# One PSUM tile of eight banks for every piece, one normalization over two banks, and another written order

## The chip, the cores and the metric

The kernel runs on one core of a Trainium2 chip. The metric is the device time of one execution in microseconds. The engines are called PE (TensorE, matmuls and transposes), DVE (VectorE), ACT (ScalarE), POOL (GpSimd) and SP (SyncE, which only issues DMAs here). Each engine has its own instruction stream and works it off in order; between engines there are semaphores.

## The reference, cut to what matters

The inputs are q, k, v of shape (4, 8, 768, 64) and the weights of a mixture of attention experts: a gate (512, 4), and for each of 4 experts wq, wk, wv (512 x 64) and wo (64 x 512). All is float32, as is the output (4, 768, 512).

```python
# first attention: 8 heads; each row sees 8 global keys and the last 96
scores = (q @ k.T) / 8 + bias            # bias = -slope[h] * distance
scores = where(keep, scores, -1e9)
a = exp(scores - max(scores)); a = a / (sum(a) + 1e-9)
x = a @ v                                # heads side by side: (4, 768, 512)
# second: 4 experts, causal, the best 2 of 4 by the gate
logits = x @ w_gate                      # w: softmax over the best two
for e in range(4):
    s = (x @ wq[e]) @ (x @ wk[e]).T / 8  # causal
    a = softmax(s)
    out += w[e] * (a @ (x @ wv[e]) @ wo[e])   # where e is among the two
```

## The kernel before

The work is cut into 24 units: 4 batches of 6 blocks of 128 rows. A unit has some forty pieces, written `name-unit`, and each piece is one or a few instructions on one engine:

- `ldq`, `ldk` (for two units at a time), `ldv`: loads, issued by SP. `cq`, `ck`, `cv` cast them to float16 (POOL, but for the first q and k). `tq`, `tk` transpose on PE, `eq`, `ek` copy the result out of PSUM (DVE).
- First attention, in halves of four heads: `s0`, `s1` are the scores on PE (before, each in a tile of two PSUM banks), `x0`, `x1` the exponentials on ACT, `m0`, `m1` the multiplication by a table of decays and masks (`M`) on DVE. `z0`, `z1` multiply by v, which has a column of ones behind it, so that each head's row sum comes out as a 65th column. `r0`, `r1` take the reciprocals of the sums and `n0`, `n1` multiply by them, both on DVE, four heads at a time (lines 641 to 666).
- `kp`, `vp` put the eight global keys and values in the place of the first rows of a used buffer; `vp` is a small DMA.
- `tx`, `ex` transpose x. `pq`, `eqk` make and copy the second q and k, `pv`, `ev` the second v and the logits; `xr`, `mx`, `wr`, `zi` make the gate's weights.
- Second attention: `s20`, `s21`, `s22` scores, `x20` to `x22` exponentials, `af` the causal mask (POOL), `y2` the product, `rz`, `cw`, `n2` the normalization with the gate's weights, `tz`, `ez`, `po`, `eo` the output projection, `so` the store.

The order is written out; a search made it: the text `ORDER` lists all pieces, and `Stream.run` issues them in that order. A word such as `eqk-1*` takes the second engine in the piece's list, and the numbers behind a colon name PSUM slots. The dictionaries of engines and times in `add` were used by the search that made the order, and decide nothing when the kernel is built, apart from the engines' order in them.

PSUM is cut into two kinds of slots: two of two banks each for scores (`s`), and four of one bank (`w`) for everything else:

```python
    def wtile(shape, dt, name):
        return psum.tile(shape, dt, name=name, tag=f"w{st.slots[0]}")

    def stile(shape, name):
        return psum.tile(shape, F32, name=name, tag=f"s{st.slots[0]}")
...
    st = Stream({"s": 2, "w": 4})
```

Ahead of all work on data, PE runs 24 matmuls of 512 columns on a tile of zeros, `nil` (`warm`, line 489). At the end `good0` to `good2` test on DVE that all row sums lie in a range (`inside`, line 792), `total` adds the results up on PE, and `flag` hands the number to a branch: if a sum is out of range, a slow general path computes all again. It is not taken here.

Of the kernel before, what the change touches and what calls it, by code (L numbers as in the profile page):

```python
# [8 lines left out]
F32 = mybir.dt.float32  # L9
# [19 lines left out]
s1-4:1 rz-0 x0-4 ldk-6 pv-1:3 cw-0 kp-4 n2-0 ldq-8 n0-2 pq-1:2 x1-4 cq-6 n1-2 ldv-6 ones mx-1 ldk-8
m1-3 eqk-1* tq-6:1 tx-2:0 m1-4 w-o z0-3:2 ex-2 s20-1:1 r0-3 s0-5:0 m0-4 pq-2:0 xr-1 x0-5 wr-1 eq-6  # L30
ck-6 ev-1 n0-3 s1-5:0 eqk-2* z1-3:2 x20-1 vp-3 m0-5 tk-6:1 ldv-4 r1-3 tz-0:0 x1-5 pv-2:3 ldk-10 ek-6
af-1 n1-3 kg-6 s0-6:1 s1-6:0 ez-0 x0-6 m1-5 tx-3:2 po-0:0 x1-6 ldq-10 kp-6 m0-6 y2-1:1 ldq-12 xr-2
eo-0 cq-8 ex-3 s21-2:1 s0-7:0 rz-1 x21-2 mx-2 pq-3:2 zi-1 ldv-7 cw-1 x0-7 cv-6 ev-2* wr-2 tq-8:0
ck-8 n2-1 eqk-3* s1-7:1 eq-8 s20-2:0 x1-7 z0-6:1 tz-1:3 m1-6 tk-8:2 cv-4 r0-6 ez-1 x20-2 z1-6:0 n0-6
s20-3:1 vg-6 r1-6 z1-4:1 n1-6 po-1:3 ck-10 vp-6 ek-8 ldv-5 s21-3:0 eo-1 r1-4 tx-6:0 n1-4 pv-3:2
x20-3 kp-7 ex-6 z0-4:3 m0-7 tk-10:1 xr-3 ev-3 vp-4 cq-10 pq-6:0 r0-4 x21-3 n0-4 ek-10 tx-4:3 af-2
zi-2 ldk-12 mx-3 s0-8:1 ex-4 s1-8:0 cq-12 ldq-14 x0-8 eqk-6 pq-4:3 m1-7 so-1 tq-12:1 eqk-4* cv-7
wr-3 tq-10:0 eq-12 x1-8 s21-4:1 eq-10 cv-5 z0-7:1 z1-7:2 x21-4 r0-7 kp-8 s20-4:0 m1-8 vp-7 z0-5:0
ldv-8 z1-5:3 x20-4 r1-7 n0-7 s22-4:1 r0-5 n1-7 y2-2:1 ck-12 r1-5 x22-4 n0-5 tx-7:2 ldk-14 n1-5
s1-9:0 s20-6:1 rz-2 tx-5:3 x20-6 cw-2 ldv-9 ex-7 tk-12:0 ldq-16 x1-9 ex-5 cq-14 s0-9:1 ek-12 pq-5:2  # L40
x0-9 zi-3 n2-2 kp-9 af-4 pv-5:3 eqk-5* m0-8 s0-10:1 tq-14:1 xr-5 af-3 mx-5 x0-10 wr-5 pq-7:2 cv-8
eq-14 ev-5 m1-9 s21-5:0 eqk-7* s1-10:1 m0-10 z1-8:3 x21-5 z0-8:1 kp-10 r1-8 tz-2:2 kg-12 y2-3:0
ck-14 r0-8 vp-8 ez-2 x1-10 n1-8 ldv-10 pv-4:2 rz-3 n0-8 ldk-16 po-2:3 cw-3 ldv-12 cv-9 tx-8:1 n2-3
eo-2 s22-5:0 so-0 ex-8 s1-11:1 xr-4 ev-4 m0-9 tz-3:0 tk-14:3 x22-5 cq-16 mx-4 pq-8:1 ez-3 ek-14
x1-11 m1-10 s1-12:0 po-3:0 x1-12 af-6 eqk-8 z1-9:3 eo-3 s0-12:1 m1-12 s20-5:0 x0-12 wr-4 z0-9:1
pv-6:0 ck-16 zi-4 x20-5 r1-9 vp-9 r0-9 n1-9 y2-4:2 ldq-18 zi-5 n0-9 xr-6 so-2 ev-6 s21-8:1 rz-4
s0-11:0 af-5 mx-6 ldk-18 x21-8 wr-6 tx-9:3 tq-16:1 cw-4 ldv-11 x0-11 kp-12 ex-9 cv-10 tk-16:0 n2-4
eq-16 s20-8:1 ldv-13 s20-7:0 x20-8 m1-11 tz-4:2 pq-9:3 ez-4 ek-16 x20-7 af-8 z0-10:1 po-4:2 m0-11
eqk-9* y2-5:0 cq-18 r0-10 eo-4 n0-10 s1-13:1 rz-5 s21-9:0 cw-5 x1-13 cv-12 z1-10:1 n2-5 tq-18:2
vp-10 r1-10 m0-12 tz-5:3 x21-9 z1-12:0 ldq-20 n1-10 s0-13:1 ez-5 so-3 pv-7:1 kp-13 eq-18 ck-18 x0-13  # L50
ldk-20 po-5:3 r1-12 mx-7 ev-7* tx-10:2 xr-7 s1-14:0 zi-6 eo-5 wr-7 s0-14:1 vg-12 x1-14 zi-7 z0-12:1
ex-10 tk-18:3 af-7 vp-12 r0-12 n1-12 pq-10:2 so-5 cv-11 x0-14 ek-18 so-4 m1-13 s20-9:0 eqk-10*
z0-11:0 kg-18 n0-12 cv-13 pv-8:3 x20-9 r0-11 n0-11 tx-12:1 kp-14 z1-11:2 cq-20 mx-8 ex-12 y2-6:0
ldv-14 xr-8 s21-10:1 ev-8 rz-6 r1-11 s0-15:0 wr-8 x21-10 n1-11 y2-7:1 pq-12:3 rz-7 cw-6 cw-7 x0-15
n2-6 n2-7 tx-11:2 tq-20:0 m0-13 eqk-12* tz-7:1 s22-10:1 ex-11 s1-15:0 x22-10 ez-7 z1-13:3 kp-15
eq-20 z0-13:2 ck-20 x1-15 tz-6:1 vp-13 s1-16:1 r1-13 ez-6 n1-13 pq-11:0 ldv-15 x1-16 m0-14 ldq-22
ldv-16 po-7:1 cv-14 r0-13 eqk-11* n0-13 po-6:3 m1-14 eo-7 s21-11:0 s22-11:1 eo-6* x21-11 pv-9:1
m0-15 tx-13:2 so-6 z0-14:0 x22-11 mx-9 s0-16:0 r0-14 ex-13 pv-10:3 kp-16 n0-14 af-9 xr-9 x0-16
z1-14:2 wr-9 y2-8:0 ev-10* cv-15 vp-14 s20-10:1 r1-14 mx-10 ev-9 ldk-22 zi-8 n1-14 s1-17:0 xr-10
x20-10 ldv-19 zi-9 tk-20:1 rz-8 wr-10 so-7 cw-8 pq-13:2 m1-15 x1-17 af-10 n2-8 y2-9:3 ek-20 cq-22  # L60
eqk-13* tz-8:0 s20-11:0 ez-8 s1-18:1 rz-9 x20-11 tx-14:1 cw-9 cv-16 po-8:0 ex-14 z0-15:2 n2-9 x1-18
z1-15:1 r0-15 ck-22 tz-9:3 n0-15 eo-8 vp-15 s20-12:0 s0-17:1 r1-15 ez-9 pq-14:2 n1-15 so-8 x0-17
zi-10 m1-16 ldv-18 tq-22:3 x20-12 m0-16 po-9:0 eqk-14* m1-18 tk-22:1 eq-22 eo-9 s0-18:0 s20-13:1
m1-17 so-9 x0-18 z0-16:2 pv-11:3 ldv-17 x20-13 kp-18 ek-22 af-12 y2-10:0 mx-11 r0-16 xr-11 ev-11
cv-18 s21-14:0 wr-11 s20-14:1 x21-14 n0-16 tx-15:1 vg-18 ldv-22 z1-16:3 rz-10 x20-14 ex-15 s1-19:0
vp-16 r1-16 cw-10 pv-12:2 n1-16 x1-19 n2-10 s0-19:1 mx-12 m0-18 tx-16:3 tz-10:0 kp-19 pq-15:1 x0-19
m0-17 ez-10 ex-16 ev-12 s1-20:0 xr-12 eqk-15 s0-20:1 x1-20 po-10:0 kp-20 m1-19 z0-18:3 pq-16:1 cv-17
x0-20 wr-12 eo-10* af-14 z1-17:2 eqk-16* r0-18 so-10 s1-21:1 n0-18 af-11 s0-21:0 ldv-20 r1-17 x1-21
z0-17:3 n1-17 cv-19 z1-18:1 zi-11 y2-12:0 r0-17 y2-11:2 r1-18 vp-18 af-13 n0-17 x0-21 ldv-23 zi-12
rz-12 n1-18 kp-21 s21-15:1 rz-11 cw-12 pv-13:1 cw-11 x21-15 n2-12 tx-17:3 n2-11 tz-12:0 mx-13  # L70
s21-16:0 ev-13 ex-17 s20-15:1 xr-13 x21-16 ez-12 pq-17:3 wr-13 m0-19 x20-15 cv-20 tz-11:0 z1-19:2
ez-11 po-12:1 r1-19 m0-21 eqk-17* po-11:0 af-15 zi-13 eo-12 s22-16:0 n1-19 s20-16:1 eo-11* z0-19:3
x22-16 so-12 y2-13:1 cv-22 pv-14:2 r0-19 x20-16 so-11 rz-13 n0-19 tx-18:0 vp-19 cw-13 mx-14 s1-22:0
n2-13 xr-14 ldv-21 ev-14 s21-17:1 ex-18 x1-22 tz-13:3 tx-19:1 wr-14 pq-18:0 ez-13 m0-20 x21-17 m1-20
pv-15:3 y2-14:2 xr-15 ex-19 eqk-18* s22-17:1 zi-14 rz-14 s20-17:0 mx-15 cw-14 ev-15 wr-15 z0-20:1
x22-17 n2-14 z1-20:0 po-13:3 r0-20 r1-20 vp-20 n0-20 y2-15:2 zi-15 eo-13 n1-20 tz-14:1 rz-15 x20-17
# [785 lines left out]
```

## Time and profile before

| | |
|---|---|
| median of 3 runs | 146.87 us (146.66 to 147.22) |
| the profiled execution | 146.58 us, span 144.9 us |
| mean granted clock of PE | 0.964 |
| busy: PE, DVE, ACT, POOL | 130.0, 120.2, 120.1, 70.2 us |
| moved by DMA | 27.83 MB, mean 192 GB/s |

The span runs from the first to the last instruction. The page gives busy time of each engine, the span in 40 slices of 3.6 us (the digits are tenths, PEclk the granted TensorE clock), the DMA queues, and the chain of work that ended last, followed back from the end. Groups of instructions are listed by line, engine and operation, with shapes (out<-in), their number, busy time and the mean of one in ns, and then the engine's idle time before them with what ended it. A table by stretches gives for each engine the busy us in that stretch, with the number of instructions. L384 is the line of the helper `copy`, so its groups are told apart by tile: `QK` is written by `eqk`, `V` by `cv` or `ev`, `wqk` by `w-q` and `w-k`. A line of an engine with a q behind its name (SPq) is time in which its sequencer held the chain.

### The profile page before, as it was taken

Reading aid. Unit: us, or ns where it says so; the run is one execution under the profiler, and the core shown is the slowest. Engines: PE = TensorE matmul, PEld = TensorE weight load, DVE = VectorE, ACT = ScalarE, POOL = GpSimd, SP = SyncE. Lnnn points to the kernel's source line nnn. Section 1 sums busy time; section 2 is a strip of 40 time slices with the busy share of each in tenths; the row PEclk is TensorE's granted clock in tenths of the full one; section 3 lists DMA queues with packets and bytes.
Section 4 is the critical chain, followed back from the end, with each engine's and each line's share of the span. In section 5 each row is a group of like instructions: output and inputs, shape, how many; then the busy total and the mean of one; then the engine's idle time right before and its main releaser. Section 6 shows DMA issues by size and latency. Waiting matters only on the chain.

```text
span 144.9 us, 5515 instructions
## 1 busy us (share of the span) xinstructions
PE 130.0 (90%) x2222; PEld 101.5 (70%) x2222; DVE 120.2 (83%) x420; ACT 120.1 (83%) x198; POOL 70.2 (48%) x116
## 2 busy tenths in 40 slices
PE   6985779697998999999999999889999999999870
PEld 2453466485877788778798787668878887978620
DVE  1257784897999989999999998989999998887870
ACT  3867766679985998988999998889999998899760
POOL 6058216534997596674773345545641370413100
PEclk9999555999999999999999999999999999999999
DMA  2999999599898997969999699770527204023164
GB/s 78 304 275 305 245 310 222 177 299 246 226 289 181 294 273 166 246 147 299 202 258 303 148 253 261 212 175 9 157 67 219 73 14 152 5 75 113 34 235 140
DMA packets 55725, 27.83 MB, mean 192 GB/s; under 512 B 26096, under 2 KB 52368, under 8 KB 55696
## 3 DMA queue, kind: packets, MB, share of 16 engines
q1 hardware_dynamic: 55696, 27.45, 72.2%
q8 instruction: 18, 0.29, 0.9%
q14 instruction: 11, 0.09, 0.2%
HBM read 20.98 MB, written 6.29 MB: 188 GB/s over the span
## 4 chain that ended last, share of the span: by engine, by line
PE 60%; DVE 14%; DMA 8%; SPq 7%; issue 3%; ACT 2%; POOL 2%; ACTq 0%
PE pq L689 13%; PE s L727 7%; PE sc L630 7%; PE pv L695 6%; PE z L647 5%; PE z L751 5%; DMA wg<-in_moe_w_gate_dram 5%; PE po L774 4%; SPq L578 4%; DMA rawqk<-in_k_dram 4%; PE tx L679 3%; PE tk L596 3%; DVE A L639 3%; PE z L650 3%; PE tq L591 3%
## 5 line engine op out<-in xcount | busy, mean ns | idle before, releaser
L634 ACT ACTIVATE A<-sc 128x1024 f16<-128x1024 f32 (+1 forms) x48 | 44.6, 960 | 6.7 <-PE sc L630 6.3
L731 ACT ACTIVATE A<-s 128x1024 f16<-128x1024 f32 (+1 forms) x48 | 43.4, 930 | 2.1 <-PE s L727 1.8
L639 DVE TENSOR_TENSOR A<-A,M 128x1024 f16<-128x1024 f16 (+1 forms) x48 | 35.0, 742 | 0.2 <-ACT A L634 0.2
L739 POOL TENSOR_SCALAR_AFFINE_SELECT A<-A 128x512 f16<-128x512 f16 x24 | 18.0, 761 | 19.6 <-ACT A L731 14.1
L689 PE MATMUL pq<-xT,wqk 128*128 128x128 f16 x384 | 26.3, 223 | 1.3 <-DVE z L761 1.2
L689 PEld LDWEIGHTS <-wqk 128*128 128x128 f16 x384 | 23.1, 100 | 2.3 <-DVE z L761 1.5
L384 POOL CAST k<-rawqk 128x1024 f16<-128x1024 f32 x11 | 15.3, 1388 | 12.7 <-DMA rawqk<-in_k_dram 12.6
L663 DVE TENSOR_TENSOR x<-z,rall 128x256 f16<-128x256 f32 x48 | 19.5, 413 | 0.4
L630 PE MATMUL sc<-qT,kT 64*128 64x128 f16 x352 | 17.4, 224 | 2.5 <-DVE kT L384 1.2
L647 PE MATMUL z<-V,A 128*128 128x65 f16 x192 | 17.1, 196 | 2.2 <-POOL V L384 1.0
L384 POOL CAST V<-rawv 128x512 f16<-128x512 f32 x24 | 15.7, 658 | 3.9 <-PE s L727 1.9
L647 PEld LDWEIGHTS <-A 128*128 128x128 f16 x192 | 13.1, 99 | 5.1 <-DVE wr L712 0.8
L727 PE MATMUL s<-QK 64*128 64x128 f16 x336 | 15.9, 219 | 0.0
L384 POOL COPY kT<-KG 128x32 f16<-128x32 f16 x20 | 5.4, 272 | 20.9 <-PE sc L630 20.9
L695 PE MATMUL pv<-wvg,xT 128*128 128x264 f16 x96 | 15.3, 283 | 0.0
L630 PEld LDWEIGHTS <-kT 64*128 64x128 f16 x352 | 11.1, 97 | 5.9 <-issue 1.9
L384 POOL CAST q<-rawqk 128x1024 f16<-128x1024 f32 x11 | 11.7, 1059 | 6.7 <-DMA rawqk<-in_q_dram 6.7
L650 PE MATMUL z<-V,A 128*128 128x65 f16 x160 | 14.6, 195 | 0.0
L384 ACT CAST QK<-pq 128x512 f16<-128x512 f32 x20 | 11.9, 595 | 2.5 <-PE pq L689 2.5
L774 PE MATMUL po<-wo,zT 128*128 128x512 f16 x48 | 13.9, 380 | 0.0
L751 PE MATMUL z<-V,A 128*128 128x65 f16 x336 | 13.8, 193 | 0.0
L751 PEld LDWEIGHTS <-A 128*128 128x128 f16 x336 | 12.3, 97 | 1.8 <-issue 0.4
(70 smaller groups left out, 226.0 us busy)
## 6 DMA issues: line engine op xcount, KB each, us to landing
rawqk<-in_q_dram SPq DMA_DIRECT2D x12, 512.0 KB
rawqk<-in_k_dram SPq DMA_DIRECT2D x12, 512.0 KB
rawv<-in_v_dram SPq DMA_DIRECT2D x24, 256.0 KB
out_dram<-o_sb SPq DMA_DIRECT2D x24, 256.0 KB
w<-in_moe_wk_dram SPq DMA_DIRECT2D x1, 512.0 KB
w<-in_moe_wq_dram SPq DMA_DIRECT2D x1, 512.0 KB
w<-in_moe_wv_dram SPq DMA_DIRECT2D x1, 512.0 KB
wo<-in_moe_wo_dram SPq DMA_DIRECT2D x1, 512.0 KB
```

Source lines behind the costliest of these rows:

```text
L384: act.copy(o, i) if e == "ACT" else (dve if e == "DVE" else pool).tensor_copy(o, i)
L630: mm(sc[:, par, pr, prev * P:(prev + 1) * P], lhsT=share(kT, u - prev)[L, p, :], rhs=share(qT, u)[L, p, :], start=True, stop=True)
L634: act.activation(A1[(2 * u + hf) % (2 * R)][:, :, :, 0:w], T.pop(("s", u, hf))[:, :, :, 0:w], func=Exp, scale=scale1)
L639: eng[e].tensor_tensor(a, a, M[:, hf, :, :, :] if ri else M0[:, hf, :, :, :], op=Alu.mult)
L647: mm(z[:, h % 4, :], lhsT=a[:, par, pr, 0:P], rhs=V1[i][:, h, 0:DV], start=True, stop=not ri)
L663: add(f"n{hf}", lambda e, hf=hf, r1=r1: dve.tensor_tensor(x16[i][:, 256 * hf:256 * hf + 256].rearrange("p (h d) -> p h d", d=Dh), T.pop((" ...
L689: mm(ps[:, j, :], lhsT=wqk[:, ko, j, :], rhs=xT[i][:, ko, :], start=(ko == 0), stop=(ko == nko - 1))
L695: mm(ps[:, :], lhsT=xT[i][:, ko, :], rhs=wvg[:, ko, :], start=(ko == 0), stop=(ko == nko - 1))
L727: mm(sc[:, par, n, :], lhsT=QK2[b % 2][L, ki, 2 + p2, :], rhs=QK2[b % 2][L, ri, p2, :], start=True, stop=True)
L731: act.activation(A2[i][:, :, 4 * ch:4 * ch + m, :], T.pop(("s2", u, ch))[:, :, 0:m, :], func=Exp, scale=scale2)
L751: mm(z[:, ex, :], lhsT=A2[i][:, ex % 2, n, :], rhs=V2[b % 2][:, ki, ex, 0:DV], start=(j == 0), stop=(j == len(mine) - 1))
L774: mm(ps[:, :], lhsT=zT[i][:, p2, :], rhs=wo[:, p2, :], start=(p2 == 0), stop=(p2 == E // 2 - 1))
```

## The change

It has five parts.

1. PSUM is one tile of eight banks. Any piece may take any bank, and a piece of two banks any two neighbours.
2. `z0`, `z1` become one piece `z` over two banks, which waits for both masks; `r0`, `r1` become one reciprocal of eight columns and `n0`, `n1` one multiplication over both banks.
3. `busy` puts matmuls of 128 columns on `nil` in front of a piece, as many as the order says behind a plus sign: 9, 26, 9, 10, 21, 10 and 7, 92 in all, before `tk-0`, `s1-0`, `s1-1`, `tk-2`, `tq-2`, `s1-2` and `pq-0`.
4. The check of the row sums is cut after unit 19, not after unit 22, and waits for the reciprocals, not the multiplications.
5. The order is another one: other places of all pieces, other engines for some copies (`eqk` 17 times on ACT and 7 on DVE, before 20 and 4; `eo` 18 and 6, before 19 and 5; `ev` 17 and 7 in both; `w-q` on DVE, before on ACT; both fills of ones on POOL), and another order of the loads.

The loads on SP's queue begin so (the numbers are MB up to and with that load):

```
before  ldq-0 0.5  ldk-0 1.0  ldq-2 1.6  ldk-2 2.1  ldv-0 2.4  ldq-4 2.9  ld-k 3.4  ld-q 3.9  ldv-1 4.2  ld-g 4.2  ld-v 4.7  ldk-4 5.3
after   ldq-0 0.5  ldv-1 0.8  ldk-0 1.3  ldv-0 1.6  ldk-2 2.1  ldq-2 2.6  ld-g 2.6  ld-k 3.2  ld-q 3.7  ldq-4 4.2  ldk-4 4.7  ldv-2 5.0  ld-v 5.5
```

The core of the diff:

```diff
-ident nil ldq-0 warm:2 ldk-0 ident32 ldq-2 dg ldk-2 iota d mask ldv-0 d0 d1 M-1-1 ldq-4 cq-0 ck-0
-ld-k M-0-0 M-1-0 tk-0:3 cq-2 tq-0:1 ek-0 ld-q M-0-1 V1one* eq-0 tq-2:2 perm kg-0 s0-0:1 ldv-1 eq-2
...
+V1one* ldq-0 nil iota warm:0 ldv-1 V2one* d ldk-0 dg mask ident d0 d1 M-0-0 ident32 perm ldv-0 cq-0
+ldk-2 M-1-0 M-0-1 ldq-2 tq-0:4 ck-0 tk-0:7+9 ld-g cv-0 ek-0 vg-0 eq-0 cv-1 s1-0:01+26 s0-0:67 ld-k
...
             name, _, slots = word.partition(":")
+            slots, _, idle = slots.partition("+")
+            self.idle = int(idle or 0)
...
-    def wtile(shape, dt, name):
-        return psum.tile(shape, dt, name=name, tag=f"w{st.slots[0]}")
-
-    def stile(shape, name):
-        return psum.tile(shape, F32, name=name, tag=f"s{st.slots[0]}")
+    banks = psum.tile([P, 8, 4 * P], F32, name="banks")
+
+    def busy(t):
+
+        for n in range(st.idle):
+            mm(t[:, 0:P], lhsT=nil[:, 0:P], rhs=nil[:, 0:P], start=True, stop=True)
+
+    def one(dt=F32):
+
+        t = banks[:, st.slots[0], :]
+        busy(t)
+        return t if dt == F32 else t.bitcast(dt)
+
+    def two():
+
+        lo, hi = st.slots
+        assert hi == lo + 1
+        busy(banks[:, lo, :])
+        return banks[:, lo:hi + 1, :]
...
-    st = Stream({"s": 2, "w": 4})
+    st = Stream({"b": 8})
...
-                T["s", u, hf] = sc = stile([P, 2, 2, 2 * P], "sc")
+                T["s", u, hf] = sc = two().rearrange("l a (r q) -> l a r q", q=2 * P)
...
-            add(f"r{hf}", lambda e, hf=hf, r1=r1: dve.reciprocal(r1, T["z", u, hf][:, :, Dh]), {"DVE": 0.09},
-                [f"z{hf}"])
-            add(f"n{hf}", lambda e, hf=hf, r1=r1: dve.tensor_tensor(
-                x16[i][:, 256 * hf:256 * hf + 256].rearrange("p (h d) -> p h d", d=Dh),
-                T.pop(("z", u, hf))[:, :, 0:Dh], r1.unsqueeze(2).to_broadcast([P, 4, Dh]), op=Alu.mult),
-                {"DVE": 0.34}, [f"r{hf}", ("tx", u - R)])
+        def z1(e):
+            T["z", u] = z = two()[:, :, 0:4 * DV].rearrange("l f (h d) -> l f h d", d=DV)
+            for h in range(H):
+                a = A1[(2 * u + h // 4) % (2 * R)][:, h % 2, h // 2 % 2, :]
+                mm(z[:, h // 4, h % 4, :], lhsT=a[:, 0:P], rhs=V1[i][:, h, 0:DV], start=True, stop=not ri)
+                if ri:
+                    mm(z[:, h // 4, h % 4, :], lhsT=a[:, P:2 * P], rhs=V1[(u - 1) % R][:, h, 0:DV],
+                       start=False, stop=True)
+
+        r1 = rall[:, u, 0:H].rearrange("p (f h) -> p f h", f=2)
+        add("z", z1, {"PE": 0.5 if ri else 0.26}, ["m0", "m1", "cv"] + ([("vp", u - 1)] if ri else []),
+            "b", [["r", "n"]] * 2)
+        add("r", lambda e: dve.reciprocal(r1, T["z", u][:, :, :, Dh]), {"DVE": 0.11}, ["z"])
+        add("n", lambda e: dve.tensor_tensor(
+            x16[i][:, :].rearrange("p (f h d) -> p f h d", f=2, d=Dh), T.pop(("z", u))[:, :, :, 0:Dh],
+            r1.unsqueeze(3).to_broadcast([P, 2, 4, Dh]), op=Alu.mult), {"DVE": 0.61}, ["r", ("tx", u - R)])
...
-    last = NU - 1
-    flat = rall[:, 0:last, :].rearrange("p u n -> p (u n)")
-    st.add("good0", inside(flat, last * (H + E), 1.0 / SUM_HI, 1.0 / SUM_LO, 0), {"DVE": 0.8},
-           [("n2", u) for u in range(last)])
...
-    st.add("good2", inside(rall[:, last, :], H + E, 1.0 / SUM_HI, 1.0 / SUM_LO, 2), {"DVE": 0.3},
-           [("n2", last), ("n0", last), ("n1", last)])
+    last, n0 = NU - 1, NU - 4
+    for n, (lo, hi) in enumerate(((0, n0), (n0, NU))):
+        st.add(f"good{2 * n}", inside(rall[:, lo:hi, :].rearrange("p u n -> p (u n)"), (hi - lo) * (H + E),
+                                      1.0 / SUM_HI, 1.0 / SUM_LO, 2 * n), {"DVE": (0.65, 0.4)[n]},
+               [("rz", u) for u in range(lo, hi)] + [("r", u) for u in range(lo, hi)])
```

The other lines of the diff put `one()` or `two()` where a piece took `wtile` or `stile`, and change the search's times.

## The prediction, as it was put on record

> **What bounds the kernel now.** I read the page first, for the engines' shares, the granted clock and the chain that ended last.
>
> ```profile
> PE 130.0 (90%) x2222; PEld 101.5 (70%) x2222; DVE 120.2 (83%) x420; ACT 120.1 (83%) x198; POOL 70.2 (48%) x116
> PEclk9999555999999999999999999999999999999999
> PE 60%; DVE 14%; DMA 8%; SPq 7%; issue 3%; ACT 2%; POOL 2%; ACTq 0%
> ```
>
> The chain is 60% PE, but PE's 90% is not 90% of its rate: a 128-column matmul is shown for 223 ns, while 16 of them (one `pq`) pass in 0.89 us in the chain, 56 ns each. DVE and ACT, 83% each, have rows that hardly overlap, so their busy time is nearly their work. The table of ten-microsecond stretches says where they are full:
>
> ```profile
> 10.00:20.00 10.00, 6.14 (x85) 4.37 (x84) 7.73 (x20) 6.85 (x8) 5.11 (x10) 0.75 1.10 284
> 20.00:30.00 10.00, 8.51 (x116) 6.76 (x114) 7.03 (x23) 5.75 (x8) 4.46 (x7) 0.74 0.85 223
> ...
> 40.00:50.00 10.00, 9.41 (x184) 7.72 (x182) 9.59 (x28) 8.02 (x12) 7.23 (x11) 1.00 1.05 258
> 50.00:60.00 10.00, 10.00 (x185) 8.49 (x182) 9.25 (x27) 9.15 (x16) 8.20 (x12) 1.00 0.90 214
> 60.00:70.00 10.00, 9.66 (x199) 7.92 (x198) 9.68 (x35) 9.12 (x15) 5.57 (x8) 1.00 0.92 242
> 70.00:80.00 10.00, 9.95 (x190) 8.27 (x190) 9.32 (x37) 9.77 (x16) 6.63 (x11) 1.00 0.95 248
> 80.00:90.00 10.00, 9.98 (x184) 7.84 (x184) 9.60 (x35) 9.55 (x16) 4.59 (x8) 1.00 0.89 219
> 90.00:100.00 10.00, 9.21 (x166) 7.07 (x160) 9.58 (x28) 8.54 (x16) 4.22 (x7) 1.00 0.61 158
> 100.00:110.00 10.00, 9.99 (x203) 8.24 (x202) 9.74 (x40) 9.99 (x17) 5.66 (x10) 1.00 0.42 119
> 110.00:120.00 10.00, 10.00 (x186) 8.44 (x184) 9.35 (x37) 9.80 (x17) 3.71 (x5) 1.00 0.29 87
> ```
>
> The columns are PE, PE's weight loads, DVE, ACT, POOL, the clock, the DMA share and GB/s. From 40 to 120 DVE works 76.1 of 80 us (95%), ACT 73.9 (92%). So there are three stages: a **start** to about 30, where ACT is idle 7.4 of 20 us and the clock is at half from 15 to 25; a **steady** stage on DVE and ACT together; and a **tail**. What the changed operations cost stands in the groups:
>
> ```profile
> L663 DVE TENSOR_TENSOR x<-z,rall 128x256 f16<-128x256 f32 x48 | 19.5, 413 | 0.4
> L661 DVE RECIPROCAL rall<-z 128x4 f32<-128x4 f32 x48 | 7.8, 171 | 0.5 <-PE z L647 0.2
> L384 DVE CAST QK<-pq 128x512 f16<-128x512 f32 x4 | 2.7, 683 | 0.9 <-PE pq L689 0.9
> L384 ACT CAST QK<-pq 128x512 f16<-128x512 f32 x20 | 11.9, 595 | 2.5 <-PE pq L689 2.5
> L384 ACT CAST wqk<-w 128x1024 f16<-128x1024 f32 x2 | 2.0, 1044 | 0.9 <-DMA w<-in_moe_wq_dram 0.9
> ```
>
> and start and tail show in the chain in order of time:
>
> ```profile
> 11.42 6.63 DMA wg<-in_moe_w_gate_dram
> ...
> 20.36 1.71 PE pq L689 x16
> ...
> 140.02 0.46 DVE ge L795 x2
> 140.62 0.30 PE pf L811 x6
> 140.95 0.15 DVE flag_i L814
> ```
>
> **The change, part by part.** The profiled execution took 146.58 us, with a span of 144.9; the median of the runs is 146.87, so 0.3 is added at the end.
>
> *Normalization over two banks.* Each of 24 units loses two reciprocals and two multiplies, 2 x (171 + 413) = 1168 ns, and gets one of each. The multiply over 128x512 is not in the trace. At least it costs the 600 ns after which DVE's next instruction starts behind a 128x512 cast, at most two of the old, 826; I take the cast's 683, since at 128x256 cast (411) and multiply (413) agree. The reciprocal of eight columns lies between 171 and 342; I take 180 (one column takes 151, four 171). So 305 ns a unit, 7.3 us; the ends are 0 and 9.5.
>
> *Who copies.* The new order has 17 `eqk` on ACT for 20, 18 `eo` for 19, and puts `w-q` on DVE. ACT loses 3 x 0.595 + 0.599 + 1.044 = 3.4. DVE gains 3 x 0.683 + 0.686, and for `w-q` 0.77 (its 128x1024 cast of k), and hands two memsets (0.16) to POOL. DVE in all: -7.3 + 2.05 + 0.69 + 0.77 - 0.16 = -4.0.
>
> *Steady stage.* Without `w-q`, DVE has 4.6 us less, ACT 2.4. If both stay as full as now, DVE's saving is worth 4.6/0.95 = 4.8 and ACT's 2.4/0.92 = 2.6. They feed each other (exponential, mask, product, normalization), so the smaller saving sets the pace: **-2.6**, between 0 and -4.8. After it ACT is the fuller of the two.
>
> *Waits.* The built streams hold more separate wait instructions: ACT 78 for 45, DVE 64 for 19 (PE 4 for 17). Nearly all the new ones let a reader of a bank wait for the bank's reader before it; PE's write in between has waited for that already, so they are met on arrival. What is queued behind each is that engine's next instruction. In the tail's chain the "issue" piece between dependent instructions is mostly 0.02 us, the whole chain's is 3% of the span, 4.3 us. So 78 more cost 0 to 78 x 0.05 = 3.9; ahead of a full engine they lie under the running instruction, so **+0.5**.
>
> *PSUM as one tile.* Scores no longer own four banks. I cost this at nothing: in the built streams the waits on banks are between accesses to the same bank, none to a neighbour. Were the cover gone, it would be the third rival below.
>
> *Start.* 92 small matmuls on zeros stand in PE's queue before `tk-0`, `s1-0`, `s1-1`, `tk-2`, `tq-2`, `s1-2` and `pq-0`. At 56 ns they are 5.1 us; between 8 and 20 us PE is idle 12 - 7.55 = 4.45 (the two-microsecond stretches), so **+0.65** if they fill it. What is behind each is the piece named, and ACT waits for the scores among these. For it the clock may stay up: from 20.0 to 25.2 PE works without a gap at half rate (`pq` 1.71 for 0.89), 5.2 us that need 2.6: **-2.6**, or nothing if the clock drops anyway. The gate weights move from 4.2 to 2.6 MB of the load queue and leave the chain; DVE stood 0.7 us for them: **-0.7**. On SP's queue 0.25 MB of v now precede the first k: by 0.5 MB in 1.85 us, k lands 0.9 later, half of it under the warm matmuls that end at 8.37: **+0.45**. Sum -2.2.
>
> The trace explains the clock only so far: it fell at 15.0, though between 8.4 and 15 the longest gap before a matmul is 0.67 us. [...]
>
> *Tail.* The last check now covers four units, so the flag ends about 1.1 us after the last `n2` instead of 2.46 (138.64 to 141.10); but the last `eo` stays 2.0 behind it, and the output transfers run at a share of 1.0 up to 142.5. **-0.4**, between 0 and -1.3.
>
> Sum: -2.2 - 2.6 + 0.5 - 0.4 = -4.7: 141.9 for such an execution, **142.2** as the median.
>
> **The rivals.**
> *More than that:* DVE's saving decides the steady stage (-4.8) and the flag the end (-1.3): -7.8, a median of 139.1. For: DVE is the fuller engine now. Against: ACT is at 9.8 to 10 from 100 to 120. Chance 0.13.
> *Slower: the fillers are paid and the clock drops all the same.* Place: PE's queue from 9 to 20. At half rate a filler is 1.71/16 = 107 ns, 92 are 9.8, less the 4.45 of idle +5.4; with -0.7 and +0.45 the start is +5.1, the sum +5.1 - 2.6 + 0.5 - 0.4 = +2.6, a median of 149.5. It decides once more than 2.8 us of fillers lie in front of ready work. For: they cannot give way, and 26 of them (1.5 us) precede the first score. Against: before `tk-0` there is idle time anyway. Chance 0.17.
> *The steady stage gives its saving back.* `z` now waits for both masks, and needs two neighbouring banks at once; before, the first half's product ran under the second mask (0.60 us). If a quarter of 24 x 0.6 shows, +3.6 takes the place of -2.6: a median of 148.4; if the saving is just lost, 144.8. For: PE takes its queue in order, with 95% of DVE taken there is little to hide it. Against: in the new order one to three other pieces of PE stand between the second mask and `z` in units 0 to 2, and four to some twenty later. Chance 0.20, half of it over 146.
> *The change does not do what it says:* one tile couples its banks. If each of the 96 score pieces waited 0.25 us, +24, about 171. The built streams have no such wait. Chance 0.01.
>
> **How the numbers follow.** The forecast has the rest, 0.49. A measurement of this kernel tells about 0.5% (0.7 us) from no change. Faster by more: 0.45 of the forecast, 0.13, and 0.06 of the third: 0.64. Within: 0.03 + 0.05 = 0.08. Slower: 0.17 + 0.09 + 0.01 + 0.01 of the forecast = 0.28. The range reaches from the first rival, 139.0, to the second, 149.5; outside lie some 0.07 below and 0.11 above. The forecast's own range is 140 to 145.
>
> **What would show it.** The clock row has no 5 after the first 8 us, and PE no gaps between 9 and 20; if the 5s stay, the second rival holds. The multiply is one row of 24 at about 683 ns, DVE near 116 and ACT near 117 us busy. In the stretches from 40 to 120 both stay over 90%; if they fall, the idle time before `z` names the third rival. If the sums hold and the time does not, transfers are the cause that I left out: up to 90 us their share is near 0.9.

## The result, and the profile after

The changed kernel takes 152.42 us (median of 4 runs, 150.7 to 153.59) where the kernel before, run beside it, takes 146.76 (146.0 to 147.22): a ratio of 1.03, interval 1.0213 to 1.0388. It is slower, and the forecast of 142.2 and its range up to 149.5 are both missed. (Ratios here are taken over undisturbed runs, so they need not equal the quotient of two medians.) The profiled execution took 151.49 us with a span of 149.7, 4.8 more than the span before.

The page of the changed kernel, the same three lines as before (busy time of each engine, the granted clock in 40 slices, the chain that ended last by engine):

```profile
PE 132.1 (88%) x2314; PEld 105.1 (70%) x2314; DVE 119.4 (80%) x375; ACT 118.1 (79%) x193; POOL 69.4 (46%) x118
...
PEclk9999999999999999999999999999999999999995
...
PE 57%; DMA 11%; ACT 10%; DVE 7%; POOL 4%; issue 4%; SPq 1%; ACTq 0%; DVEq 0%
```

In this execution the clock does not fall before the end, as forecast. DVE, which was to lose 4.0 us, lost 0.8; ACT lost 2.0 for the forecast 3.4. The groups of DVE that the merge touches:

```profile
L673 DVE TENSOR_TENSOR x<-banks,rall 128x512 f16<-128x512 f32 x24 | 16.5, 686 | 0.4
...
L672 DVE RECIPROCAL rall<-banks 128x8 f32<-128x8 f32 x24 | 4.8, 201 | 3.4 <-PE banks L666 2.4 <-PE banks L664 0.5 <-ACT A L648 0.3
```

The multiplication takes 686 ns (forecast 683) and the reciprocal 201 (180): the durations were right. Their idle time is not: before, DVE stood 0.5 us in front of its 48 reciprocals, now 3.4 us in front of 24, 2.9 of them for the product on PE.

The table by stretches of the changed kernel (PE, weight loads, DVE, ACT, POOL, clock, DMA share, GB/s):

```profile
0.00:40.00 40.00, 34.34 (x510) 25.99 (x511) 26.04 (x64) 27.67 (x50) 20.59 (x46) 1.00 0.99 237
...
40.00:60.00 20.00, 16.94 (x297) 13.61 (x295) 18.39 (x48) 17.80 (x25) 14.15 (x19) 1.00 1.00 243
60.00:80.00 20.00, 19.14 (x371) 16.02 (x371) 18.18 (x66) 16.66 (x30) 10.71 (x16) 1.00 0.78 212
80.00:100.00 20.00, 19.65 (x378) 15.94 (x375) 18.74 (x45) 18.88 (x26) 12.40 (x20) 1.00 0.71 185
100.00:120.00 20.00, 19.37 (x384) 16.15 (x381) 17.97 (x60) 19.38 (x31) 5.95 (x11) 1.00 0.55 143
120.00:140.00 20.00, 19.87 (x371) 16.27 (x369) 17.78 (x84) 15.74 (x32) 5.64 (x9) 1.00 0.19 69
140.00:155.00 15.00, 2.79 (x30) 1.08 (x26) 2.27 (x14) 1.98 (x4) 0.00 (x0) 0.79 0.26 92
```

and the rows of the kernel before that the prediction does not show:

```profile
0.00:40.00 40.00, 31.85 (x394) 22.40 (x394) 26.77 (x77) 28.66 (x50) 20.24 (x44) 0.87 0.97 244
...
120.00:140.00 20.00, 19.60 (x357) 14.91 (x356) 16.72 (x85) 16.83 (x33) 4.13 (x6) 1.00 0.22 81
140.00:155.00 15.00, 0.31 (x7) 0.21 (x6) 0.60 (x3) 0.69 (x2) 0.00 (x0) 0.93 0.18 65
```

From 40 us until its last work PE runs at full clock in both kernels (1.00 in each stretch to 140), so PE's busy time that is still to come at 40 says how far each has got: 98.1 us before (130.0 less 31.9), 97.75 after (132.1 less 34.3). The start has thus gained only 0.4 us. The rest is PE standing idle after that (stretch less PE's busy time):

| stretch | PE idle before | after | difference |
|---|---|---|---|
| 40 to 60 | 0.59 | 3.06 | +2.5 |
| 60 to 120 | 1.20 | 1.84 | +0.6 |
| 120 to 140 | 0.40 | 0.13 | -0.3 |
| 140 to the end | 4.55 | 6.87 | +2.3 |

With -0.4 that is the 4.8 us. The share of DVE from 40 to 120 fell from 95 to 92%, that of ACT from 92 to 91%, that of PE from 98 to 94%: nothing got fuller, and PE got emptier. What PE waited for, by the waits of the changed kernel (line waited at, releaser, us in all, times, longest):

```profile
...
PE banks L778 <- DVE z L770: 1.2, 2, 0.9
PE banks L644 <- DVE qT L398: 1.1, 1, 1.1
PE banks L736 <- DVE x L673: 0.9, 2, 0.7
PE banks L605 <- POOL q L398: 0.9, 1, 0.9
PE banks L666 <- DMA V<-VG: 0.7, 1, 0.7
PE banks L778 <- DVE kT L398: 0.6, 1, 0.6
```

L778 is `tz`, L644 a score of the first attention, L736 one of the second, L605 `tq`. The merged product (L664, L666) is nearly absent: 0.7 us for a `vp` in the start and 0.4 us elsewhere. The long waits lie between 40 and 60 and are for DVE. `tz` waits from 40.9 to 41.8 for `n2`: DVE had stood 0.77 us for the merged product, up to its reciprocal at 37.9, and worked from there to `n2` without a gap. A score waits from 53.0 to 54.1 for `eq-10`, which stands on DVE behind `eq-12`, and both stand behind two masks. From the timeline, which merges rows of a kind (start, us, engine):

```profile
50.18 2.68 DVE L653 TENSOR_TENSOR A<-A,M 128x1024 f16<-128x1024 f16 x2
52.78 1.28 DVE L398 COPY qT<-banks 128x1024 f16<-128x1024 f16 x2
...
50.58 3.47 POOL L398 CAST k<-rawqk 128x1024 f16<-128x1024 f32 x2
```

These two masks took 0.99 and 1.76 us, where most of this size take 0.68. All masks over 0.95 us, six in the kernel before and seven in the changed one, lie beside a cast on POOL for at least 0.4 us, though not every mask beside a cast is slow. That the casts slow them is not isolated by a run. But the excess of these two, 1.4 us, is more than the score's wait of 1.1: in the new order a slow pair falls where PE has nothing else to do.

Start and end in the chain of the changed kernel, in order of time (start, us, what):

```profile
9.16 0.50 PE banks L379 x9
...
10.11 1.45 PE banks L379 x26
...
11.89 0.61 PE banks L379 x9
...
13.05 0.66 PE banks L379 x10
...
14.24 1.17 PE banks L379 x21
...
17.02 4.22 DMA rawqk<-in_k_dram
...
22.24 2.87 DMA V<-VG
...
61.47 6.27 DMA rawqk<-in_q_dram
...
137.97 3.85 DMA out_dram<-o_sb
...
142.40 0.60 ACT o_sb L398
...
143.00 0.58 ACT o_sb L398
```

L379 are the fillers: 75 of the 92 lie on the chain, 4.39 us, where the forecast had 0.65. At the end `eo-22` waits 1.6 us for the store of unit 18, and three output copies stand between 141.9 and 143.59, where the last `eo` ends (before 140.69). The span ends 6.07 us after it (before 4.17).

### The profile page after: what moved, and what is told of

Its sections match the earlier page's. It is cut to its first block, busy times and chain, and to the rows that moved or that the text cites. A ratio compares the mean times of both kernels' runs of the same rounds, so it can differ in the third digit from the quotient of the medians.

```text
span 149.7 us, 5718 instructions
## 1 busy us (share of the span) xinstructions
PE 132.1 (88%) x2314; PEld 105.1 (70%) x2314; DVE 119.4 (80%) x375; ACT 118.1 (79%) x193; POOL 69.4 (46%) x118
## 4 chain that ended last, share of the span: by engine, by line
PE 57%; DMA 11%; ACT 10%; DVE 7%; POOL 4%; issue 4%; SPq 1%; ACTq 0%; DVEq 0%
PE banks L698 10%; PE banks L736 6%; PE banks L644 6%; PE banks L783 5%; PE banks L704 5%; PE banks L507 5%; PE banks L760 4%; DMA rawqk<-in_q_dram 4%; ACT A L740 4%; PE banks L664 4%; ACT A L648 3%; PE banks L379 3%; DMA rawqk<-in_k_dram 3%; DMA out_dram<-o_sb 3%; PE banks L688 3%
## 5 line engine op out<-in xcount | busy, mean ns | idle before, releaser
L648 ACT ACTIVATE A<-banks 128x1024 f16<-128x1024 f32 (+1 forms) x48 | 44.4, 957 | 8.6 <-PE banks L644 8.2
L740 ACT ACTIVATE A<-banks 128x1024 f16<-128x1024 f32 (+1 forms) x48 | 42.6, 920 | 9.1 <-PE banks L736 7.7
L748 POOL TENSOR_SCALAR_AFFINE_SELECT A<-A 128x512 f16<-128x512 f16 x24 | 15.8, 669 | 21.9 <-ACT A L740 21.8
L698 PE MATMUL banks<-xT,wqk 128*128 128x128 f16 x384 | 25.4, 219 | 0.3 <-ACT A L648 0.2
L644 PE MATMUL banks<-qT,kT 64*128 64x128 f16 x352 | 16.5, 217 | 2.3 <-DVE qT L398 1.1
L736 PE MATMUL banks<-QK 64*128 64x128 f16 x336 | 15.7, 218 | 1.3 <-DVE x L673 0.9
L673 DVE TENSOR_TENSOR x<-banks,rall 128x512 f16<-128x512 f32 x24 | 16.5, 686 | 0.4
L644 PEld LDWEIGHTS <-kT 64*128 64x128 f16 x352 | 10.8, 94 | 6.4 <-issue 4.4
L664 PE MATMUL banks<-V,A 128*128 128x65 f16 x192 | 14.2, 194 | 0.4 <-ACT A L740 0.2
L783 PE MATMUL banks<-wo,zT 128*128 128x512 f16 x48 | 14.0, 381 | 0.4 <-DVE zT L398 0.3
L704 PE MATMUL banks<-wvg,xT 128*128 128x264 f16 x96 | 14.1, 277 | 0.1
L760 PE MATMUL banks<-V,A 128*128 128x65 f16 x336 | 14.0, 193 | 0.2
L736 PEld LDWEIGHTS <-QK 64*128 64x128 f16 x336 | 10.4, 94 | 4.8 <-issue 2.1
L664 PEld LDWEIGHTS <-A 128*128 128x128 f16 x192 | 12.1, 97 | 2.0 <-issue 0.8
L666 PE MATMUL banks<-V,A 128*128 128x65 f16 x160 | 12.4, 193 | 0.7 <-DMA V<-VG 0.7
```

Source lines behind the costliest of these rows:

```text
L644: mm(sc[:, par, pr, prev * P:(prev + 1) * P], lhsT=share(kT, u - prev)[L, p, :], rhs=share(qT, u)[L, p, :], start=True, stop=True)
L648: act.activation(A1[(2 * u + hf) % (2 * R)][:, :, :, 0:w], T.pop(("s", u, hf))[:, :, :, 0:w], func=Exp, scale=scale1)
L664: mm(z[:, h // 4, h % 4, :], lhsT=a[:, 0:P], rhs=V1[i][:, h, 0:DV], start=True, stop=not ri)
L673: add("n", lambda e: dve.tensor_tensor(x16[i][:, :].rearrange("p (f h d) -> p f h d", f=2, d=Dh), T.pop(("z", u))[:, :, :, 0:Dh], r1.unsqu ...
L698: mm(ps[:, j, :], lhsT=wqk[:, ko, j, :], rhs=xT[i][:, ko, :], start=(ko == 0), stop=(ko == nko - 1))
L704: mm(ps[:, :], lhsT=xT[i][:, ko, :], rhs=wvg[:, ko, :], start=(ko == 0), stop=(ko == nko - 1))
```

## The experiments

### What can be taken back one by one

**One tile alone.** The kernel before, its order and its slots, in one tile:

```diff
+    banks = psum.tile([P, 8, 4 * P], F32, name="banks")
     def wtile(shape, dt, name):
-        return psum.tile(shape, dt, name=name, tag=f"w{st.slots[0]}")
+        t = banks[0:shape[0], 4 + st.slots[0], :]
...
```

> The kernel before with nothing changed but that its eight banks are one tile (same slots, same order, same pieces). Theory A (the new order and its loads cost the time): 146.8, within 0.7 of before, and no chain piece that waits for another bank. Theory B (one tile couples the engines' readers): 149 or more, with idle time on ACT and DVE in the steady stage.

146.04 us, a ratio of 0.9981 (0.994 to 1.0023). One tile costs nothing, as forecast.

**The fillers.** The changed kernel, the numbers behind the plus signs removed.

```diff
-... tk-0:7+9 ... s1-0:01+26 ... s1-1:45+9 ... tk-2:6+10 ... tq-2:4+21 ... s1-2:23+10 ... pq-0:4+7
+... tk-0:7 ... s1-0:01 ... s1-1:45 ... tk-2:6 ... tq-2:4 ... s1-2:23 ... pq-0:4
```

> The changed kernel without its 92 small matmuls. If they lie on the chain and cost more than the clock gives (4.4 us of them stand in its chain): faster than the changed kernel by 1 to 3, the clock at half for one stretch of 10 us. If the clock is worth more than they cost: slower than it by 1 to 2.5, and 0.5 in the clock row.

151.28 us, 1.0336 (1.0211 to 1.0461): like the changed kernel. The clock line of this run has the half clock back:

```profile
PEclk9996555999999999999999999999999999999995
```

In this pair the clock stays up with the fillers, and they bring no time that the runs can tell. With the same start it does not always stay up: it fell to half for 3.4 us in the profiled executions of two runs below, at 20.4 with the late check (mean granted clock 0.980) and at 25.9 with eight output buffers (0.971; changed kernel 0.986).

**The early check.** The changed kernel with the check cut after unit 22 again and `total` and `flag` behind the last `eo`.

```diff
-    last, n0 = NU - 1, NU - 4
+    last, n0 = NU - 1, NU - 1
```

> The changed kernel with the check of before: cut after unit 22, the long part last, so that the flag comes after the last copy of an output. Theory D (the early branch fetches instructions while the last stores run, and their last packets are late): 1 to 2 us faster than the changed kernel, last store packets over within 2.2 us of the last issue. If D is wrong: the same or up to 1 us slower.

150.81 us, 1.0275 (1.016 to 1.039). The end behind the last `eo` shrinks from 6.07 to 4.43 us in the profiled execution, but the last `eo` moves from 143.59 to 144.96. Of the 5 us, 0.4 (by the ratios) to 1.6 (by the medians) would be here; the intervals overlap, so no gain is shown.

**The halves on DVE.** The changed kernel, order and banks kept; `r` makes two reciprocals and `n` two multiplications. The changed kernel ran beside it as a control.

```diff
-        add("r", lambda e: dve.reciprocal(r1, T["z", u][:, :, :, Dh]), {"DVE": 0.11}, ["z"])
+        def r(e):
+            for hf in range(2):
+                dve.reciprocal(r1[:, hf, :], T["z", u][:, hf, :, Dh])
...
+            for hf in range(2):
+                dve.tensor_tensor(x16[i][:, 256 * hf:256 * hf + 256]...
```

> The changed kernel again, unaltered, beside the other three on this chip: 151 to 153.5 us by every theory. It is what the next two are compared with.

> The changed kernel, its order and its banks, with only the DVE work of a unit cut again: r makes two reciprocals of four columns, n two multiplications of 256 columns. This puts back what the forecast counted at 24 x 305 ns = 7.3 us of DVE. Theory A (DVE sets the time of the steady stage and the merge saves there, the loss is elsewhere): 3 to 7 us above the changed kernel. Theory B (two multiplications of which the second starts 0.33 us after the first cost DVE hardly more than the one of 686 ns, and DVE has slack): within 1 us of the changed kernel.

The control took 151.89 us, the halves 151.74, with ratios of 1.0369 (1.0297 to 1.044) and 1.0376 (1.029 to 1.0463). Putting the halves back costs nothing that these runs can tell, within about 1 us, and the saving is smaller than forecast. DVE is busy 122.0 us with the halves and 119.4 in the control: 2.6 us, 108 ns a unit for the forecast 305. The groups with the halves:

```profile
L679 DVE TENSOR_TENSOR x<-banks,rall 128x256 f16<-128x256 f32 x48 | 17.9, 414 | 0.0
...
L674 DVE RECIPROCAL rall<-banks 128x4 f32<-128x4 f32 x48 | 6.6, 168 | 1.8 <-PE banks L666 1.1 <-PE banks L664 0.3
```

48 x 414 ns would be 19.9 us; the group is busy 17.9. In the trace the second multiplication of a pair starts 334 ns after the first, while the first is still shown as running, and the instruction behind a merged one starts 608 ns after it. So two halves hold DVE 668 ns and one whole 608, a difference of 60, not 2 x 413 - 683 = 143; the rest of the 108 is the reciprocal's (6.6 us in its rows, in the changed kernel 4.8).

**A load.** In the changed kernel `ldq-18` could start at 46.8 and was issued at 61.5, behind `vp-8`, and the chain holds 6.27 us of it.

```diff
-vp-8 ... ldq-18 ... ldv-10
+ldq-18 ldv-10 vp-8
```

> The changed kernel with two words moved: ldq-18 and ldv-10 ahead of vp-8 on the queue of SP. In the changed kernel ldq-18 could start at 46.8 us and was issued at 61.5, behind vp-8, and the chain of waits then holds 6.27 us of its transfer. Theory A (that load behind vp-8 is the loss between 50 and 70 us): 149 to 150 us, 1.5 to 2.7 below the changed kernel. Theory B (unit 18 is only the last of several late pieces there, and DVE and POOL hold the stretch all the same): within 1 us of the changed kernel.

151.91 us, no change. The load has left the chain, and other waits stand in its place: here the longest link of the chain was not a cause.

**The output buffers.** The changed kernel with eight `o_sb`.

```diff
-    o_sb = ring(R, [P, Dm], F32, "o_sb")
+    o_sb = ring(2 * R, [P, Dm], F32, "o_sb")
```

> The changed kernel with eight buffers o_sb for the output in place of four, so that eo-22 waits for no store (in the changed kernel it stood 1.6 us for the store of unit 18 to land, and the chain of waits holds 3.85 us of that store). Theory A (the early flag lets the fetch of the branch's code delay that store, and so the last three stores bunch; this is the 2 us by which the end behind the last eo grew): 149.5 to 150.5 us, 1.5 to 2 below the changed kernel's 151.9. Theory B (the output transfers themselves are the end, and leave later whatever the buffers): within 0.7 us of 151.9.

151.48 us, no change. No `eo` waits for a store any more, but PE has work up to 144.1, and the last `eo` ends at 144.80. In this execution (152.63 us) the tail is late with PE, and not for want of buffers.

### What the engines' work is worth

Three loads were added to the kernel before, each alone, and one was taken away (that run leaves out a part of the output: the second two experts in units 2 to 21).

```diff
+            for n in range(6 if 5 <= u <= 20 else 0):                      # more PE, in pq
+                mm(ps[:, 0, :], lhsT=nil[:, 0:P], rhs=nil[:, 0:P], start=True, stop=True)
...
+            if 5 <= u <= 17:                                               # more DVE, in ex
+                copy(e, spare[:, :].rearrange("p (k q) -> p k q", q=P), t[:, :, :])
...
+            if 7 <= u <= 16:                                               # more ACT, in eqk
+                act.copy(spare[:, :].rearrange("p (k q) -> p k q", q=P), t[:, :, :])
...
-            for p2 in range(E // 2):                                       # less PE, in po
+            half = 1 if 2 <= u <= 21 else E // 2
+            for p2 in range(half):
```

> The kernel before with PE work added and nothing else: six matmuls of 128 columns on zeros ahead of pq of units 5 to 20, 96 x 56 ns = 5.4 us in the steady stage. Theory A (the premise of the forecast: DVE and ACT set the pace, PE is not at its rate): 146.8 to 148.8 us, at most 2 above the kernel before. Theory B (PE sets the pace from 40 us on): 151 to 152.5 us, nearly all of the 5.4. Theory C (no engine alone does; the order is tight on all three): 149 to 152.

> The kernel before with DVE work added and nothing else: a second copy of tx into a spare buffer that nobody reads, behind ex of units 5 to 17, 13 x 418 ns = 5.4 us. Theory A (DVE, 95% busy, sets the pace): 150.5 to 152.5 us, 70 to 100% of it. Theory B (PE sets it, and DVE has slack): 146.5 to 148.5 us. Theory C (tight on all): 149 to 152.

> The kernel before with ACT work added and nothing else: a second copy of pq into a spare buffer that nobody reads, behind eqk of units 7 to 16, 10 x 595 ns = 5.9 us. Theory A (ACT, 92% busy, sets the pace with DVE): 151 to 153 us. Theory B (PE sets it, and ACT has slack): 146.5 to 148.5 us. Theory C (tight on all): 149 to 152.

> The kernel before with PE work taken away: po of units 2 to 21 makes one matmul of 512 columns in place of two, so the second two experts' part of the output is left out there; 20 x 0.22 = 4.4 us of PE. Theory A (PE is the bound, and what is taken from it comes off the time as what was added came on, 0.8 for each): 142.3 to 143.5 us. Theory B (with each engine's order fixed, work taken away is given back in the next wait on another engine, as with DVE's and ACT's): 145 to 146.8 us.

| | work by its rows | median | change of the medians | ratio | cost of 1 us, by the ratio's interval |
|---|---|---|---|---|---|
| more PE | +5.4 us | 150.14 | +4.4 | 1.0333 (1.0225 to 1.0441) | 0.6 to 1.2 |
| more DVE | +5.4 | 147.31 | +1.5 | 1.0115 (1.0035 to 1.0195) | 0.1 to 0.5 |
| more ACT | +5.9 | 149.73 | +4.0 | 1.024 (1.0134 to 1.0346) | 0.3 to 0.9 |
| less PE | -4.4 | 146.27 | -0.7 | 0.9916 (0.9837 to 0.9995) | 0.0 to 0.5 |

The first three stood beside runs of before at 145.77, the fourth beside runs at 146.96. By the medians an added us of PE costs 0.8, of ACT 0.67, of DVE 0.28. A us taken from PE brings back 0.16 by the medians and 0.28 by the ratio (-1.2 us). The interval of added PE lies above those of DVE and of removed PE; that of ACT overlaps with its neighbours. The added copies on DVE and ACT also read a bank of PSUM once more and so hold it longer; how much of their cost is the bank's is not separated. The stretch from 40 to 120 us in the table by stretches (columns as above), first of the kernel before:

```profile
40.00:120.00 80.00, 78.22 (x1471) 63.99 (x1468) 76.11 (x257) 73.95 (x117) 45.82 (x68) 1.00 0.75 193
```

of more PE:

```profile
40.00:120.00 80.00, 79.08 (x1510) 66.36 (x1504) 71.56 (x248) 72.17 (x113) 44.58 (x67) 1.00 0.74 188
```

of more DVE:

```profile
40.00:120.00 80.00, 78.17 (x1468) 63.94 (x1466) 77.36 (x270) 74.15 (x116) 46.06 (x68) 1.00 0.76 193
```

and of more ACT:

```profile
40.00:120.00 80.00, 75.61 (x1410) 61.86 (x1408) 71.66 (x248) 74.76 (x122) 43.47 (x67) 1.00 0.75 191
```

More PE makes DVE and ACT emptier (76.1 to 71.6 and 74.0 to 72.2), while more DVE leaves PE as full as it was, and more ACT empties both PE and DVE (78.2 to 75.6 and 76.1 to 71.7). So PE comes before DVE among the limits, and by these stretches ACT does too, though PE's 90% is not 90% of its rate and DVE shows the higher share of the two others.

**Work moved from ACT to DVE, and the clock, in the old order.** The kernel before as one tile, in one run with `eqk` of six units on DVE for ACT, in one with 71 fillers only where PE had idled between 9 and 20, in one with both.

```diff
-eqk-5* ... eqk-9* ... eqk-11* ... eqk-13* ... eqk-16* ... eqk-18*
+eqk-5 ... eqk-9 ... eqk-11 ... eqk-13 ... eqk-16 ... eqk-18
...
+tq-2:2+9 s1-0:0+9 s0-1:1+10 z1-0:2+4 s0-2:0+4 tq-4:1+8 tx-0:0+8 z1-1:1+13 z0-1:3+6
```

> The kernel before as one tile, with eqk of units 5, 9, 11, 13, 16 and 18 on DVE in place of ACT: ACT loses 6 x 0.595 = 3.6 us, DVE gains 6 x 0.683 = 4.1 us. Theory A (an added us of DVE costs 0.28 us and one of ACT 0.67, as the two added loads showed, and a removed one gives the same): 144.2 to 145.6 us, some 1.2 below 146.0. Theory B (what is added costs and what is taken away gives nothing, since PE is at its limit): 146 to 148 us.

> The kernel before as one tile (same slots and order, 146.0 us), with 71 matmuls of 128 columns on zeros put only where PE stood idle between 9 and 20 us, in number 80 to 90% of each gap: 9 ahead of tq-2, 9 s1-0, 10 s0-1, 4 z1-0, 4 s0-2, 8 tq-4, 8 tx-0, 13 z1-1, 6 z0-1; 71 x 56 ns = 4.0 us. Theory A (the clock holds and the gaps take them): 143.8 to 145 us, 1 to 2.3 below. Theory B (each filler delays what follows, or the start waits for loads and not for PE): 145.5 to 147.5 us.

> The two edits before this one together, in the kernel before as one tile: 71 fillers in PE's gaps of the start, and six eqk on DVE. Theory A (both gain): 142.5 to 144.5 us. Theory B (neither does): 146 to 148 us.

The copies: 148.61 us, 1.0155 (1.0109 to 1.0202), slower by 2.3. ACT has 3.6 us less by the rows, DVE 4.1 more; by the table that should have been about -1.2.

The fillers: 146.63 us, 0.998 (0.9932 to 1.0027), with the clock at full throughout:

```profile
PEclk9999999999999999999999999999999999999997
```

Even in PE's idle gaps, at no visible price, the held clock brings at most 1 us. Both together: 148.0, 1.0075 (1.0027 to 1.0123). The stretch from 40 to 120, first with the fillers alone (an execution of 144.41 us), then with both (147.72):

```profile
40.00:120.00 80.00, 79.22 (x1517) 65.81 (x1514) 76.05 (x265) 75.11 (x120) 44.58 (x66) 1.00 0.77 196
...
40.00:120.00 80.00, 77.30 (x1461) 63.75 (x1459) 77.07 (x263) 70.34 (x109) 45.47 (x67) 1.00 0.76 192
```

ACT gets emptier by 4.8 us and PE by 1.9. The six copies stand on DVE where the order had left no room for them; which waits behind them make the loss was not followed.

### The merge, in the old order and in the new

**Old order.** First the banks handed out freely (each piece takes the bank whose last reader stands earliest) with the halves apart, then the same with `z`, `r` and `n` merged at the place of the later half (for which one exponential, `x1-21`, had to go behind `z-17`).

```diff
-z1-8:3 ... z0-8:1 ... r1-8 ... r0-8 ... n1-8 ... n0-8
+z1-8:7 ... z0-8:0 ... r1-8 ... r0-8 ... n1-8 ... n0-8      # banks free, halves apart
+z-8:67 ... r-8 ... n-8                                      # banks free, merged
```

> The order of the kernel before, all eight banks handed out freely (each piece takes the bank whose last reader stands earliest in the order), the halves z0, z1, r0, r1, n0, n1 left apart as before. Theory A (the 8.4 us that the merged form lost in this order come from merging: z waits for both masks and holds two banks from the first matmul to the last multiplication): 146 to 148 us, like the kernel before. Theory B (they come from handing out the banks freely: a piece meets a bank whose reader is late): 151 to 155 us.

> The order of before, with one tile, banks given out to any piece, and z, r, n merged over two banks (z at the place of the later half); no fillers, the check cut after unit 22. Theory A: 143 to 147, since DVE loses some microseconds and nothing else changes. Theory B (the merged normalization waits for the second mask and stalls PE): 149 to 152, as slow as the changed kernel.

Freely handed out banks: 149.22 us, 1.0168 (1.0095 to 1.0242), 2.4 above the runs of before beside it. Merged: 154.62, 1.0588 (1.0475 to 1.0702), 8.4 above. So the merge costs some 5 to 6 us where the order was not made for it. Its waits of PE from 62 to 118 us, where L664 is the merged product, L648 the exponential of the first scores and L740 that of the second:

```profile
PE banks L664 <- ACT A L648: 1.8, 2, 1.1
PE banks L664 <- ACT A L740: 1.1, 2, 0.8
PE banks L644 <- ACT A L740: 1.1, 3, 0.6
PE banks L698 <- ACT A L740: 0.5, 1, 0.5
```

By the releasers in this view the product waits not for masks (DVE) but for banks: two neighbours are wanted, and an exponential still reads the scores in one.

**New order, merge undone.** Two forms. In the first, the half whose mask comes first has its product, reciprocal and multiplication early; in the second, only its product is early, and DVE's order is kept.

```diff
-m1-8 ... m0-8 ... z-8:45 ... r-8 ... n-8
+m1-8 ... m0-8 ... z1-8:2 r1-8 n1-8 ... z0-8:5 ... r0-8 ... n0-8     # first form
+m1-8 ... m0-8 ... z1-8:4 ... z0-8:5 ... r1-8 r0-8 ... n1-8 n0-8     # second form
```

> The changed kernel with the merge undone altogether and its order otherwise kept: in every unit the product of the half whose mask comes first stands about two PE pieces behind that mask (2 to 34 words ahead of the old place of z), in any bank that is free there, with its own reciprocal and multiplication; the other half stays where z, r and n stood. Theory A (what the changed kernel loses between 40 us and the end comes from z waiting for both masks and for two banks): 147 to 149.5 us, 2.5 to 5 below the changed kernel's 151.9. Theory B (the new order itself is what PE waits on, with or without the merge): 151 to 153 us.

> The run before that put half-products early lost 31 us since its early reciprocals stood in DVE's queue ahead of their products (DVE waited 17.9 us there), so it told nothing of z. Here the changed kernel's DVE order is kept (both reciprocals where r stood, both multiplications where n stood, as in the run with halves, 151.7 us), and only the product of the half whose mask comes first stands ahead, 2 to 18 words before z, one to four PE pieces, in a free bank. Theory A (the new order loses because z waits for both masks and takes two banks at once): 147.5 to 150 us. Theory B (z hardly waits in the new order, PE stood 0.6 us for it in all, and other pieces make PE wait): 151 to 153.5 us.

182.72 us (180.01 to 185.0) and 162.48 (1.1079, 1.0995 to 1.1164): far worse than the 152 that they were to mend. In the first form the early reciprocals hold DVE's queue:

```profile
DVE rall L677 <- PE banks L671: 17.9, 18, 1.8
```

In the second the early product (L668) takes banks that come free in the order before they do in time:

```profile
PE banks L668 <- ACT A L652: 4.1, 4, 1.1
PE banks L668 <- ACT A L746: 3.5, 6, 0.9
```

Neither isolates the wait for both masks, which stays untested by itself. They show that the new order has no room for these two earlier places of a product. The mild form, halves on DVE alone, is the one that tells something of the merge in the new order, and it is neutral.

## Why the prediction was wrong, step by step

**The premise of the steady stage failed.** "They feed each other, so the smaller saving sets the pace: -2.6", if both "stay as full as now". They did not stay as full. The work that the merge takes from DVE is worth nothing visible in the new order (halves), taking work from ACT onto DVE costs 2.3 us in the old one, and PE, set aside as not at its rate, is the engine on which added work costs most by the medians. The condition was the error: what a saving is worth cannot be read from a share of busy time. DVE, at 95%, paid 0.28 us for an added one. That an engine with less to do waits in the same places, since the order is fixed, is a reading that no run shows by itself. From 40 to 120 PE idled 3.1 us more; forecast was -2.6 with +0.5 for waits.

**Normalization** was right in its mechanism and mis-sized: 2.6 us of DVE, not 7.3, since the sum took 2 x 413 ns where the two follow each other at 334. The premise that DVE's rows hardly overlap was wrong for the profile before, too: there the next instruction mostly starts 331 ns after such a multiplication, which is shown for 413. The forecast used the 600 ns spacing for the whole, as a lower end, and not the spacing for the halves.

**Start:** forecast -2.2, measured -0.4 up to 40 us. The clock step (-2.6) held in kind, since the 5s are gone from this execution, and the fillers' +0.65 was too small, since it set them against PE's idle gaps of the old order. The new order puts them in front of ready scores: 4.39 us of the chain. Without fillers the time is the same. The old order with fillers only in its gaps shows more: the held clock itself brings 1 us at most. That small matmuls ahead of PE's work would keep the clock up was the author's estimate, which the trace of before, without any, could not show. In the run without fillers the clock fell at 12.2, with PE busy 0.46 of the 2 us from 10 to 12.

**Tail:** forecast -0.4, measured +2.0 from 120 us on, 1.8 of it in the landing of the last stores. PE has work to do until the last microseconds, so the flag's place could not shorten it. The earlier flag is visible: the last packets of the instruction queues run from 145.0 to 146.3, among the last stores, which land until 147.27, 3.7 us after the last `eo`; before, they began at 143.0, behind stores that had landed at 142.58, 1.9 us after it, and with the late check at 146.95 (landed 147.04, 2.1 us after it). Larger buffers, and the late check, bring nothing that the runs can tell, so mending this alone is not enough.

**One tile at nothing** was right. **Who copies** was right in its counts, and ACT lost 2.0 us for 3.4. The price of the separate **waits** was not tested.

**The rivals.** Half of the second happened: the fillers are paid (4.39 us of the chain), but in the profiled execution the clock held. The third named z's waiting, with 148.4 us. In the order before it is the nearest to what the runs show, by the bank half of its sentence ("needs two neighbouring banks at once"), and dearer than forecast. In the new order the product waits for almost nothing.

**What stays open.** Every part that could be taken back by itself (one tile, fillers, check, DVE's merge, a load, the output buffers) gives back at most 1.6 us of 5 by the medians. What is left is the new order together with the merged product that it was made around. That it is the cause is argued by elimination, and its places are shown (PE's waits for DVE between 40 and 60, and the tail); no run repaired it. One such place is not enough: without fillers PE idles 1.5 us between 40 and 60 in place of 3.1, and the time is the same. Two parts of the new order were not taken back: its three more `eqk` on DVE, of a kind of which six cost 2.3 us in the old order, and the order of the loads beyond the one that was moved. No version tried that gives the whole output beats the kernel before by more than its runs scatter.

## What to carry to other kernels

Before a saving on a busy engine is counted, add a known load to each engine, one at a time: the slopes (here 0.8, 0.67 and 0.28, with wide intervals) say in three runs what shares of 90, 83 and 83% did not. Take one away, too: on PE a removed us brought back at most 0.5, where an added one cost at least 0.6. Price an instruction by the distance to the next start, not by its shown duration, when two of a kind follow each other (here 334 ns beside a shown 414). A merge that holds two neighbouring banks paid some 5 to 6 us for them in the old order: look for what else reads them.

## What the runs showed of the hardware

The time at half clock differs between executions of the same start. In the kernel before, the granted clock was at half for 10.2 us, from 15.00 to 25.24; PE had been busy 4.11 of the 6.60 us from 8.40 to 15.00, with no gap over 0.67 us. In the runs with more and with less PE it was at half for 6.8 us, and in the same order as one tile for 3.4, in the row

```profile
PEclk9999977999999999999999999999999999999998
```

It stayed at full where PE was busy 6.60 of those 6.60 us, in the changed kernel, and 8.03 of the 10 us from 10 to 20, in the run with fillers in the gaps. No run shows what decides it.

A bank that was free in the order was not always free in time: eight banks handed out by the order alone cost 2.4 us with unchanged work and unchanged places.
